# Halving the first layer's tiles at the start of a fused retention and SoLU kernel, with four output buffers and new operation orders

## The chip, the cores and the metric

The kernel runs on one core of one Trainium2 chip. The metric is the device time in microseconds (us) of one execution. Engines are named as in the profile: PE (TensorE matmul), PEld (its weight load), DVE (VectorE), ACT (ScalarE), POOL (GpSimd), SP (the engine that issues nearly all transfers).

## The reference

Eight batches of eight heads, 576 positions, head size 64; the result is then 4608 tokens of 512 numbers, which pass through two layers.

```python
scores = scale * np.matmul(q, k.transpose(0, 1, 3, 2))
ret = scores * Dmat[None]                 # Dmat: gamma_h ** (i - j) for i >= j, else 0
x = np.matmul(ret, v)                     # -> 4608 tokens x 512
h = x @ w_in                              # 512 -> 1024
e = np.exp(h - h_max); sm = e / (sum(e) + 1e-09)
solu = h * sm
ln = (solu - mu) / np.sqrt(var + 1e-06) * g_ln
out = ln @ w_out                          # 1024 -> 512
```

The kernel leaves out `h_max` and the division by the sum, which only scale a row that is normalised afterwards; a count of the sums of exponentials at the end decides whether the result holds or a general path must run.

## The kernel before

**Tiling.** The work is cut into 18 windows (a batch and 256 of its positions; the last 64 positions of four batches form one window). Each window has two halves of four heads, numbered i = 0 to 35, and two tiles of 128 tokens, numbered t = 0 to 35; window w has i and t = 2w and 2w + 1.

**Operations of a half i.** `ldq`, `ldk`, `ldv` load 256 KB each into raw buffers (five of each kind). `sq` and `sk` (L394, mostly POOL, a few on DVE) scale q and k by the decay, `cv` (L399) casts v. `T` transposes q and k on PE; `Te` or `TL` copies that to SBUF on ACT. `K` multiplies k and v for the running state, `st` (DVE, L554 to L557), `sm` (POOL, L562) and `sc` (POOL, L571) update and cast the state. `S` (L508) makes the scores in the one PSUM buffer named "s", `mask` (DVE, L540) applies the mask and frees it. `I` and `V` (L472) form the output in the one buffer named "xy", and `xe` (ACT, L576) copies it into `xT`.

**Operations of a tile t.** `M1_t` (L587) is the first layer: eight matmuls of 128x512 into the one PSUM buffer `h` of 128x1024, which spans two banks of 512 columns. `ex` (ACT, L595) takes the exponential of all 1024 columns and their sum, `so` (DVE, L605 for tiles 0 to 3, with a sum, else L610) multiplies h by it and so frees h. The variance comes from `va` (ACT, L624) and `fin` (DVE, L639) for tiles 0 to 3 and from `bnA`, `bnB` (DVE, L616) for the others, with `fx` (ACT, L633) and `rs` (POOL, L648 and L650) behind. `L` transposes the result, `Le` or `TL` copies it out. `M2_t` (L660) is the second layer, eight matmuls into a buffer "s" (some late tiles into "xy"), `oe` (ACT, L669) scales and copies it, `out` (SP) stores it. The last tile's M2 is cut in two, `M2_35` and `M3`, with `oe35` and `oz`.

**Weights.** `lwi0` to `lwi3` and `lwo0` to `lwo6` load 512 KB each. `wi` casts w_in into f16 (L706), a half on ACT (a), the other on DVE (b). `wg` (L710, L714) scales w_out, `WM` (L720) forms its mean, and `wc` (DVE, L728) subtracts it, so M2_0 needs all eight `wc`.

**What sets the order.** `plan()` (L122) lists all operations with durations, inputs and buffers. Each engine runs its own queue in order. `FIRST` (L42) gives each engine's order by hand up to about M1_14, `LAST` (L77) from about M1_32, and between them a key per operation does. `order_ops` (L233) walks the queues and gives each operation a planned start; the operations are written out by that start (L851 to L867), and matmuls on zeros (`fill`, L844) go into the planned gaps of PE ahead of M2_0. Two operations are skipped in that loop (L866) and written at the end:

```python
            if o.name not in ("oz", f"out{NT - 1}"):
                emit(o)
...
    with cmp.Else():
        o_ev(NT - 1, 1)
        store(NT - 1)
```

`cnt`, `cs` and `ci` form the count that the branch reads.

Of the kernel before, what the change touches and what calls it, by code (L numbers as in the profile page):

```python
# [17 lines left out]
for _b in range(0, B, 4):  # L18
# [9 lines left out]
    ldx=0.88, ldw=1.36, out=0.65,  # L28
# [7 lines left out]
CAP = dict(  # L36
    rawq=5, rawk=5, rawv=5, q16=3, k16=4, v16=4, ev=8, s=1, ret=2, xy=1, gg=6, gt=2, s160=4, s161=9, h=1,
    e=2, solu=4, osb=3, tl=1, tlx=2, tlT=1, tlL=1, wst=5,
# [4 lines left out]
    PE=(  # L43
# [5 lines left out]
    ),  # L49
    ACT=(  # L50
# [4 lines left out]
    ),  # L55
    DVE=(
# [5 lines left out]
    ),  # L62
    POOL=(
# [4 lines left out]
    ),  # L68
    SP=(
# [23 lines left out]
        "out27 out28 out29 out30 out31 out32 out33 out34 out35"  # L93
# [19 lines left out]
def late(t):  # L113
    return t + LAG >= 37
# [7 lines left out]
def plan():  # L122
# [42 lines left out]
    for t in range(NT):  # L165
# [20 lines left out]
        op(f"L{t}", "PE", "Lw" if early else "L", [f"so{t}"] + after, (m + 2, 0.1),  # L186
# [5 lines left out]
        op(f"M2_{t}", "PE", "M2h" if end else "M2", need, (t + LAG, 3.1), [("h" if end else "xy" if late(t) and t % 2 else "s", [f"oe{t}"])])  # L192
# [14 lines left out]
    op("G", "PE", "G", [], (-9999, 0.0), [("h", ["gc"])])  # L207
# [5 lines left out]
    op("cs", "PE", 0.1, ["cnt"], (NT + 2, 3.2), [("h", ["ci"])])  # L213
# [95 lines left out]
def kernel(  # L309
# [48 lines left out]
    se = const.tile([P, NT], FP)  # L358
# [222 lines left out]
    def mm1(t):  # L581
        w, c = divmod(t, 2)
        tk[t]["h"] = h_ps = pools["h"].tile([P, DFF], FP, tag="h", name="h_ps")
        for half in range(2):
            hh = slice(half * 512, half * 512 + 512)
            for dc in range(4):
# [5 lines left out]
    def exp_(t):
        d = tk[t]
        d["e"] = pools["e"].tile([P, DFF], FP, tag="e", name="e_sb")
        nc.scalar.activation(out=d["e"], in_=d["h"], func=ACT.Exp, accum_out=se[:, t : t + 1])  # L595

    def solu(t):
        d = tk[t]
        w, c = divmod(t, 2)
        d["solu"] = pools["solu"].tile([P, DFF], F16, tag="solu", name="solu")  # L600
        if c == 0:
            ws[w]["mv"] = pools["sml"].tile([P, 2, 2], FP, tag="mv", name="mv")
        if t in VA:
            d["su"] = pools["sml"].tile([P, 1], FP, tag="su", name="su")
            nc.vector.scalar_tensor_tensor(  # L605
                out=d["solu"], in0=d["h"], scalar=1.0, in1=d["e"], op0=ALU.mult, op1=ALU.mult,
                accum_out=d["su"],
            )
        else:
            nc.vector.tensor_tensor(out=d["solu"], in0=d["h"], in1=d["e"], op=ALU.mult)  # L610
# [9 lines left out]
    def squares(t):  # L620
# [4 lines left out]
            out=x, in_=d["solu"], func=ACT.Square, bias=d["su"], scale=-1024.0,  # L625
# [119 lines left out]
    def count_b():  # L745
        cur["cs"] = t = pools["h"].tile([P, DFF], FP, tag="h", name="cs")
        nc.tensor.matmul(out=t[0:1, 0:1], lhsT=cur["n"], rhs=small[:, 68:69], start=True, stop=True)

    def emit(o):
# [29 lines left out]
        elif k_ == "gc":  # L779
            nc.vector.tensor_copy(out=gln, in_=cur["g"][:, 0:8])  # L780
# [18 lines left out]
    with tc.manual_schedule():  # L799
# [30 lines left out]
        def busy(firsts, lasts):  # L830
# [9 lines left out]
            (lambda: pools["h"].tile([P, DFF], FP, tag="h", name="wm")[:, 0:512],  # L840
             busy(["G"], ["gc"]) + [(a, b + 0.7) for a, b in busy([f"M1_{t}" for t in n_t], [f"so{t}" for t in n_t])]),
# [119 lines left out]
```

## Time and profile before

| | us |
|---|---|
| median of three runs | 212.88 |
| lowest, highest | 212.33, 213.75 |
| the profiled execution | 212.58 |
| its span in the trace | 210.9 |
| PE busy | 200.8 (95%) |
| DVE busy | 166.1 (79%) |
| ACT busy | 141.7 (67%) |
| POOL busy | 141.7 (67%) |
| PE busy on zeros (L846, 41 matmuls into tl) | 12.7 |

Busy shares are averages over a start, in which loads arrive and PE has waits, a long middle, in which PE is full, and a short end. A slice of the page is 210.9 / 40 = 5.3 us. In a row of the timeline the numbers are start and duration, then engine, line, operation, output <- inputs, shapes and count; brackets hold the idle time before it and what ended it. `M1` starts (from the timeline): M1_0 15.59, M1_1 22.08, M1_2 28.72, M1_3 33.68, M1_4 41.33, M1_5 48.44, M1_6 53.44, M1_7 58.66, M1_8 63.83; from M1_8 on a tile takes about 4.9 to 5.1 us.

### The profile page before, as it was taken

Reading aid. Unit: us, or ns where it says so; the run is one execution under the profiler, and the core shown is the slowest. Engines: PE = TensorE matmul, PEld = TensorE weight load, DVE = VectorE, ACT = ScalarE, POOL = GpSimd, SP = SyncE. Lnnn points to the kernel's source line nnn. Section 1 sums busy time; section 2 is a strip of 40 time slices with the busy share of each in tenths; the row PEclk is TensorE's granted clock in tenths of the full one; section 3 lists DMA queues with packets and bytes.
Section 4 is the critical chain, followed back from the end, with each engine's and each line's share of the span. In section 5 each row is a group of like instructions: output and inputs, shape, how many; then the busy total and the mean of one; then the engine's idle time right before and its main releaser. Section 6 shows DMA issues by size and latency. Waiting matters only on the chain. (4 is left out here: it accounts for less than half of the span.)

```text
span 210.9 us, 10171 instructions
## 1 busy us (share of the span) xinstructions
PE 200.8 (95%) x4400; PEld 113.2 (54%) x4400; DVE 166.1 (79%) x279; ACT 141.7 (67%) x235; POOL 141.7 (67%) x240
## 2 busy tenths in 40 slices
PE   7986989999999999999999999999999999999992
PEld 2442654665566555555555555555666555554451
DVE  6565779997868898978898898889988998753760
ACT  2375787897666776776666777666767777573752
POOL 7434758999997975948787979797979792001110
PEclk9999999999999999999999999999999999999999
DMA  5999999999666559778999686776355222311224
GB/s 157 345 355 334 329 311 269 301 293 306 195 188 188 169 139 278 217 214 259 314 288 305 198 252 183 217 234 181 94 152 153 54 57 67 71 63 54 101 101 104
DMA packets 64814, 42.66 MB, mean 202 GB/s; under 512 B 3320, under 2 KB 58624, under 8 KB 64768
## 3 DMA queue, kind: packets, MB, share of 16 engines
q1 hardware_dynamic: 64528, 41.82, 68.4%
q8 instruction: 34, 0.56, 1.2%
q10 hardware_dynamic: 240, 0.18, 0.5%
q14 instruction: 12, 0.10, 0.2%
HBM read 32.55 MB, written 9.44 MB: 199 GB/s over the span
## 5 line engine op out<-in xcount | busy, mean ns | idle before, releaser
L587 PE MATMUL h_ps<-w_in,xT 128*128 128x512 f16 x288 | 68.5, 380 | 0.0
L660 PE MATMUL o_ps<-w2c,ev 128*128 128x512 f16 (+1 forms) x296 | 67.6, 373 | 0.0
L610 DVE TENSOR_TENSOR solu<-h_ps,e_sb 128x1024 f16<-128x1024 f32 x32 | 39.2, 1223 | 16.7 <-ACT e_sb L595 16.5
L595 ACT ACTIVATE e_sb<-h_ps 128x1024 f32<-128x1024 f32 x36 | 36.8, 1023 | 21.9 <-PE h_ps L587 20.4
L540 DVE TENSOR_TENSOR ret<-s_ps,masks 128x1024 f16<-128x1024 f32 x36 | 43.9, 1220 | 6.0 <-PE s_ps L508 5.4
L660 PEld LDWEIGHTS <-ev 128*128 128x128 f16 x296 | 28.7, 98 | 32.7
L616 DVE BATCH_NORM_STATS2 bs<-solu 128x6 f32<-128x512 f16 x64 | 43.6, 685 | 0.9
L587 PEld LDWEIGHTS <-xT 128*128 128x128 f16 x288 | 25.3, 98 | 29.1 <-ACT xT L576 0.8
L394 POOL TENSOR_TENSOR q<-rawq,small 128x512 f16<-128x512 f32 x34 | 35.4, 1042 | 7.3 <-DMA rawq<-in_q_dram 5.9
L669 ACT ACTIVATE o_sb<-o_ps,rs 128x512 f32<-128x512 f32 (+1 forms) x37 | 25.0, 676 | 21.8 <-PE o_ps L660 10.4
L394 POOL TENSOR_TENSOR k<-rawk,small 128x512 f16<-128x512 f32 x34 | 35.4, 1042 | 6.0 <-DMA rawk<-in_k_dram 5.9
L457 ACT COPY ev<-tl 128x1024 f32<-128x1024 f32 (+1 forms) x32 | 29.7, 932 | 4.7 <-PE tl L429 4.2
L576 ACT CAST xT<-xy 128x512 f16<-128x512 f32 x36 | 26.7, 742 | 3.0 <-PE xy L472 2.9
L571 POOL CAST sbd<-gg 64x256 f16<-64x256 f32 x64 | 25.4, 397 | 3.0
L562 POOL TENSOR_TENSOR gg<-gt,small 128x128 f32<-128x128 f32 x32 | 13.1, 409 | 16.9 <-DVE gt L557 16.5
L648 POOL TENSOR_TENSOR w<-mv,w 128x2 f32<-128x2 f32 x16 | 3.1, 194 | 27.8 <-ACT w L633 13.9
L399 POOL CAST v<-rawv 128x512 f16<-128x512 f32 x28 | 17.1, 609 | 0.2
L508 PE MATMUL s_ps<-ev 64*64 64x128 f16 x576 | 14.8, 218 | 0.3
L472 PE MATMUL xy<-ret,v 64*64 64x128 f16 x576 | 14.7, 217 | 0.0
L472 PEld LDWEIGHTS <-sbd 128*128 128x128 f16 x128 | 9.3, 98 | 9.3 <-issue 1.1
L446 PE MATMUL tl<-ident,solu 64*64 64x64 f16 x1024 | 14.2, 195 | 0.0
L846 PE MATMUL tl<-zeros 128*128 128x512 f16 x41 | 12.7, 445 | 1.3 <-DVE zeros L802 1.3
(71 smaller groups left out, 214.6 us busy)
## 6 DMA issues: line engine op xcount, KB each, us to landing
rawq<-in_q_dram SPq DMA_DIRECT2D x32, 256.0 KB, 5.1
rawk<-in_k_dram SPq DMA_DIRECT2D x32, 256.0 KB, 5.3
rawv<-in_v_dram SPq DMA_DIRECT2D x32, 256.0 KB, 5.1
out_dram<-o_sb SPq DMA_DIRECT2D x26, 256.0 KB, 3.1
out_dram<-o_sb SPq DMA_DIRECT2D x19, 128.0 KB, 2.3
wst<-in_moe_w_in_dram SPq DMA_DIRECT2D x4, 512.0 KB, 6.8
wst<-in_moe_w_out_dram SPq DMA_DIRECT2D x4, 512.0 KB, 7.1
rawq<-in_q_dram SPq DMA_DIRECT2D x16, 64.0 KB, 2.4
```

What stands on the lines that cost most here:

```text
L394: eng.tensor_tensor(out=t.rearrange("p j h d -> p h j d"), in0=st[i]["r" + nm], in1=g, op=ALU.mult)
L457: nc.scalar.copy(out=t[:, lo:hi].rearrange("p x (r w) -> p r x w", r=2), in_=tls[n].rearrange("p r x w -> p (r x w)").bitcast(FP).rearrang ...
L472: nc.tensor.matmul(start=(c, e) not in begun, stop=False, skip_group_check=True, **kw)
L540: nc.vector.tensor_tensor(out=d["ret"].rearrange("p e h j q -> p (e h) (j q)"), in0=d["s"].rearrange("p e h j q -> p (e h) (j q)"), in1=ma ...
L571: nc.gpsimd.tensor_copy(out=t[ee[e], :, :, ee[e]], in_=st[i]["gg"][ee[e]])
L576: nc.scalar.copy(out=xT[:, 2 * w : 2 * w + 2, 2 * hf : 2 * hf + 2].rearrange("p c h (q j) -> p c h j q", j=2), in_=xys[i][:, :, 0:256].rea ...
L587: nc.tensor.matmul(out=h_ps[:, hh], lhsT=xT[:, t, dc], rhs=w_in16[:, dc, hh], start=(dc == 0), stop=(dc == 3),)
L595: nc.scalar.activation(out=d["e"], in_=d["h"], func=ACT.Exp, accum_out=se[:, t : t + 1])
L610: nc.vector.tensor_tensor(out=d["solu"], in0=d["h"], in1=d["e"], op=ALU.mult)
L616: nc.vector.bn_stats(out=d["bs"][:, half], in_=d["solu"][:, half * 512 : half * 512 + 512])
L660: nc.tensor.matmul(out=o, lhsT=d["ev"][:, d["lo"] + c], rhs=w2c16[:, c, mm], start=(c == 0), stop=(c == 7))
L669: nc.scalar.activation(out=d["osb"][:, mm], in_=d["o", half], func=ACT.Copy, scale=ws[t // 2]["rs"][:, t % 2 : t % 2 + 1])
```

## The change

The first six tiles go through the first layer in two halves of 512 columns, each with its own product, exponential and multiplication: `M1_t`, `ex`, `so` for the first half and `Mb_t`, `ey`, `sp` for the second. `sg` (POOL) adds the two halves' sums. Tile 0's product is cut once more: `Ma0` does the part of heads 0 to 3 (two of the four steps) for both halves, ahead of M1_0 and Mb_0. h is one tile for the whole kernel, and the plan follows its two banks as `ha` and `hb`. There are four output buffers (`osb`) instead of three, and `FIRST` and `LAST` are new.

```diff
+NH, HX, ND = 6, 6, 1
-    ... s161=9, h=1, e=2, solu=4, osb=3, ...
+    ... s161=9, ha=1, hb=1, e=2, solu=4, osb=4, ...
```

Of `FIRST`, the stretches that the prediction uses (PE, ACT and POOL around M2_0, SP from the start):

```diff
 PE
-"... M1_3 T5 K7 T6 I4 S5 V4 T7 I5 S6 V5 T8 M1_4 I6 S7 V6 K8 T9 L2 M2_0 I7 L3 V7 K9 S8 M1_5 M2_1 I8 L4 V8 K10 S9 T10 M1_6"
-"M2_2 I9 L5 V9 S10 K11 T11 M1_7 M2_3 I10 L6 V10 S11 K12 T12 M1_8 ..."
+"K0 T0 S0 T1 K1 I0 V0 S1 T2 I1 S2 V1 K2 Ma0 M1_0 Mb_0 T3 K3 M1_1 I2 S3 V2 Mb_1 I3 V3 T4 L0 K4 S4 M1_2"
+"K6 Mb_2 L1 K5 M1_3 T5 K7 Mb_3 I4 V4 S5 WM I5 V5 T6 S6 I6 M1_4 T7 Mb_4 T8 S7 V6 K8 L2 T9 M2_0 I7 V7"
+"K9 S8 M1_5 L3 Mb_5 M2_1 L4 I8 T10 V8 S9 K10 M1_6 M2_2 I9 L5 V9 K11 S10 T11 M1_7 M2_3 I10 L6 V10 K12 T12 S11 M1_8 ..."
 ACT
+"cv0 Te0 cv1 Te1 wi0a xe0 Te2 wi1a cv2 xe1 wi2a wi3a ex0 cv3 ey0 Te3 ex1 xe2 cv4 ey1 xe3 Te4 cv6 Le0"
+"cv5 ex2 ey2 wg0 Le1 wg6 cv7 ex3 Te5 wg4 wg2 ey3 xe4 fx0 va1 xe5 Te6 va3 va0 Te7 ex4 Te8 xe6 ey4 va2 ..."
 DVE
+"... sp2 st5 wg7 wg1 st7 so3 wg5 wg3 mask5 sp3 wc6 wc1 wc3 wc4 wc2 mask6 wc5 wc7 wc0 mask7 fin0 so4 ..."
 POOL
-"... sk4 sq4 sk6 sm4 sc4 sk5 sm6 sk7 sm5 sq5 sc5 sq6 sq7 sk8 sq8 sk9 sc6 cv8 sq9 sm7 sc7 rs0 ..."
+"sk0 sk1 sm0 sc0 sq2 sm1 sc1 sq3 sm2 sc2 sq4 sm3 sc3 sk4 sq5 sk6 sm4 sg0 sk5 sk7 sc4 sm6 sm5 sc5 sm7"
+"sq6 sg1 sc6 sc7 cv8 sk8 sq7 sq8 sk9 sq9 cv9 rs0 ..."
 SP
-"ldq0 ldk0 ldv0 ldv1 ldq1 ldk1 lwi1 lwi2 lwi0 lwi3 ldk2 ldv2 ldq2 ldk3 ldq3 ldv3 lwo4 lwo0 ldk4 ldq4"
-"ldv4 lwo6 ldk6 lwo2 ldv6 ldk5 ldv5 ldk7 ldq5 ldv7 ldq6 ldk8 ldq7 ldq8 ldk9 ldv8 ldq9 ..."
+"ldv0 ldq0 ldk0 ldk1 ldq1 ldv1 ldk2 lwi0 ldq2 ldv2 lwi1 lwi2 lwi3 ldq3 ldk3 ldv3 ldq4 ldk4 ldv4 ldq5"
+"ldk6 ldv6 ldv5 ldk7 ldk5 lwo0 lwo6 ldv7 lwo4 lwo2 ldv8 ldq6 ldk8 ldq7 ldq8 ldk9 ldq9 ..."
```

`LAST`:

```diff
 PE
-"... M1_34 L32 M2_30 L33 L34 M1_35 M2_32 M2_33 L35 cs M2_34 M2_35 M3"
+"... M1_34 L32 L33 M2_30 M1_35 M2_33 M2_32 L35 L34 cs M2_35 M3 M2_34"
 ACT
-"... ex35 oe32 Le34 oe33 Le35 fx17 oe34 oe35 oz"
+"... ex35 fx16 oe33 Le35 fx17 Le34 oe32 oe35 oz oe34"
 DVE
-"... bnB34 cnt so35 bnA35 ci bnB35"
+"... so35 bnB34 cnt bnA35 bnB35 ci"
 SP
-"out27 out28 out29 out30 out31 out32 out33 out34 out35"
+"out27 out28 out29 out31 out30 out33 out32 out35 out34"
```

The functions:

```diff
+    sums = const.tile([P, 2, NT], FP)
+    se = sums[:, 0]
+    part = const.tile([P, 2, NH or 2, 2], FP)
+    h_ps = pools["h"].tile([P, DFF], FP, tag="h", name="h_ps")
...
+    def mm1(t, hs, dcs=range(4)):
+        for hh in hs:
+            for dc in dcs:
                 nc.tensor.matmul(
+                    out=h_ps[:, hh], lhsT=xT[:, t, dc], rhs=w_in16[:, dc, hh], start=(dc == 0), stop=(dc == 3)
                 )
...
+        hh = halves[half] if t < HX else slice(0, DFF)
+        acc = part[:, 0, t, half : half + 1] if t < HX else se[:, t : t + 1]
+        nc.scalar.activation(out=tk[t]["e"][:, hh], in_=h_ps[:, hh], func=ACT.Exp, accum_out=acc)
...
+    def sums_of(w):
+        nn = slice(0 if 2 * w < HX else 1, 2 if 2 * w in VA else 1)
+        tt = slice(2 * w, 2 * w + 2)
+        nc.gpsimd.tensor_tensor(out=sums[:, nn, tt], in0=part[:, nn, tt, 0], in1=part[:, nn, tt, 1], op=ALU.add)
```

`solu` is halved in the same way. The loop that skips `oz` and `out35` and the Else branch stay as they are.

More of the change, by code (lines that the diff above doesn't have):

```diff
@@ L36 @@
 CAP = dict(
-    rawq=5, rawk=5, rawv=5, q16=3, k16=4, v16=4, ev=8, s=1, ret=2, xy=1, gg=6, gt=2, s160=4, s161=9, h=1,
-    e=2, solu=4, osb=3, tl=1, tlx=2, tlT=1, tlL=1, wst=5,
+    rawq=5, rawk=5, rawv=5, q16=3, k16=4, v16=4, ev=8, s=1, ret=2, xy=1, gg=6, gt=2, s160=4, s161=9, ha=1, hb=1,
+    e=2, solu=4, osb=4, tl=1, tlx=2, tlT=1, tlL=1, wst=5,
 )
@@ L78 @@
     PE=(
-        "I34 L30 V34 S35 M1_32 I35 L31 V35 M2_28 M1_33 M2_29 M2_31 M1_34 L32 M2_30 L33 L34 M1_35 M2_32 M2_33 "
-        "L35 cs M2_34 M2_35 M3"
+        "I34 L30 V34 S35 M1_32 I35 L31 V35 M2_28 M1_33 M2_29 M2_31 M1_34 L32 L33 M2_30 M1_35 M2_33 M2_32 L35 "
+        "L34 cs M2_35 M3 M2_34"
     ),
     ACT=(
-        "oe27 xe34 ex32 Le30 Le31 oe28 xe35 ex33 fx15 oe29 ex34 Le32 oe30 Le33 oe31 fx16 ex35 oe32 Le34 oe33 "
-        "Le35 fx17 oe34 oe35 oz"
+        "fx15 oe27 xe34 ex32 Le31 oe28 xe35 ex33 oe29 Le30 ex34 Le33 oe31 Le32 oe30 ex35 fx16 oe33 Le35 fx17 "
+        "Le34 oe32 oe35 oz oe34"
     ),
     DVE=(
-        "so31 mask35 bnA31 so32 bnB31 bnA32 so33 bnB32 so34 bnA34 bnA33 bnB33 bnB34 cnt so35 bnA35 ci bnB35"
+        "so31 mask35 bnA31 so32 so33 bnA33 bnB31 bnA32 bnB33 so34 bnA34 bnB32 so35 bnB34 cnt bnA35 bnB35 ci"
     ),
@@ L168, in plan @@
         va = t in VA
-        op(f"M1_{t}", "PE", "M1", [f"xe{2 * w}", f"xe{2 * w + 1}"] + [f"wi{x}{y}" for x in range(4) for y in "ab"], (m, 1.4), [("h", [f"so{t}"])])
-        op(f"ex{t}", "ACT", "ex", [f"M1_{t}"], (m, 3.3), [("e", [f"so{t}"])])
-        op(f"so{t}", "DVE", "soA" if va else "so", [f"ex{t}"], (m, 4.56), [("solu", [f"L{t}", f"va{t}" if va else f"bnB{t}"])])
+        xs = [f"xe{2 * w}", f"xe{2 * w + 1}"] + [f"wi{x}{y}" for x in range(4) for y in "ab"]
+        out = f"sp{t}" if t < NH else f"so{t}"
@@ new lines, in plan @@
+        solu = [("solu", [f"L{t}", f"va{t}" if va else f"bnB{t}"])]
+        hs = [("ha", [f"so{t}"]), ("hb", [out])]
+        if t < ND:
+            op(f"Ma{t}", "PE", "M1h", [f"xe{2 * w}"] + [f"wi{x}{y}" for x in range(2) for y in "ab"], (m, 1.0), hs)
+            xs.append(f"Ma{t}")
+        got = ["", ""] if t < ND else hs
+        if t < NH:
+            op(f"M1_{t}", "PE", "M1q" if t < ND else "M1h", xs, (m, 1.4), [x for x in got[:1] if x])
+            op(f"Mb_{t}", "PE", "M1q" if t < ND else "M1h", [f"M1_{t}"], (m, 2.3), [x for x in got[1:] if x])
+            if t < HX:
+                op(f"ex{t}", "ACT", "exh", [f"M1_{t}"], (m, 2.5), [("e", [out])])
+                op(f"ey{t}", "ACT", "exh", [f"Mb_{t}"], (m, 3.4))
+            else:
+                op(f"ex{t}", "ACT", "ex", [f"M1_{t}", f"Mb_{t}"], (m, 3.3), [("e", [out])])
+            op(f"so{t}", "DVE", "soB" if va else "soh", [f"ex{t}"], (m, 3.3 if t < HX else 4.5), solu)
+            op(out, "DVE", "soB" if va else "soh", [f"ey{t}" if t < HX else f"ex{t}"], (m, 4.2 if t < HX else 4.7))
+        else:
+            op(f"M1_{t}", "PE", "M1h" if t < ND else "M1", xs, (m, 1.4), [x for x in got if x])
+            op(f"ex{t}", "ACT", "ex", [f"M1_{t}"], (m, 3.3), [("e", [out])])
+            op(out, "DVE", "soA" if va else "so", [f"ex{t}"], (m, 4.56), solu)
@@ L172, in plan @@
+        sums = t < HX or t < NH and va
+        if sums and c:
+            op(f"sg{w}", "POOL", "sg", ([f"ey{t - 1}", f"ey{t}"] if t < HX else []) + ([f"sp{t - 1}", f"sp{t}"] if va else []), (m, 4.9))
         if va:
-            op(f"va{t}", "ACT", "va", [f"so{t}"], (m + 1, 0.8))
+            op(f"va{t}", "ACT", "va", [f"sg{w}" if sums else out], (m + 1, 0.8))
         else:
-            op(f"bnA{t}", "DVE", "bnA", [f"so{t}"], (m + 1, 0.9))
+            op(f"bnA{t}", "DVE", "bnA", [out], (m + 1, 0.9))
@@ L185, in plan @@
         after += [f"Le{t - 2}"] if t - 2 >= NS - 6 else []
-        op(f"L{t}", "PE", "Lw" if early else "L", [f"so{t}"] + after, (m + 2, 0.1),
+        op(f"L{t}", "PE", "Lw" if early else "L", [out] + after, (m + 2, 0.1),
            [("tlL" if early else "tl" if jn else "tlx", [ev_L(t)])])
@@ L579, in x_ev @@
         )
[L581 to L586, printed above, removed]
+    halves = [slice(0, 512), slice(512, 1024)]
+    def mm1(t, hs, dcs=range(4)):
+        for hh in hs:
+            for dc in dcs:
                 nc.tensor.matmul(
-                    out=h_ps[:, hh], lhsT=xT[:, t, dc], rhs=w_in16[:, dc, hh],
-                    start=(dc == 0), stop=(dc == 3),
-                )
@@ L592, in exp_ @@
[L592 to L597, printed above, removed]
+                    out=h_ps[:, hh], lhsT=xT[:, t, dc], rhs=w_in16[:, dc, hh], start=(dc == 0), stop=(dc == 3)
+                )
+    def exp_(t, half=0):
+        if not half:
+            tk[t]["e"] = pools["e"].tile([P, DFF], FP, tag="e", name="e_sb")
+        hh = halves[half] if t < HX else slice(0, DFF)
+        acc = part[:, 0, t, half : half + 1] if t < HX else se[:, t : t + 1]
+        nc.scalar.activation(out=tk[t]["e"][:, hh], in_=h_ps[:, hh], func=ACT.Exp, accum_out=acc)
@@ L598, in solu @@
+    def solu(t, half=0):
         d = tk[t]
         w, c = divmod(t, 2)
-        d["solu"] = pools["solu"].tile([P, DFF], F16, tag="solu", name="solu")
-        if c == 0:
-            ws[w]["mv"] = pools["sml"].tile([P, 2, 2], FP, tag="mv", name="mv")
+        if not half:
+            d["solu"] = pools["solu"].tile([P, DFF], F16, tag="solu", name="solu")
+            if c == 0:
+                ws[w]["mv"] = pools["sml"].tile([P, 2, 2], FP, tag="mv", name="mv")
+        hh = halves[half] if t < NH else slice(0, DFF)
@@ L655, in mm2 @@
         nm = "xy" if half or late(t) and t % 2 else "s"
-        nm = "h" if t == NT - 1 and not half else nm
         mm = slice(256 * half, 256 * half + (256 if t == NT - 1 else DM))
-        d["o", half] = o = pools[nm].tile([P, 2, 512], FP, tag=nm, name="o_ps")[:, 0, 0 : mm.stop - mm.start]
+        if t == NT - 1 and not half:
+            o = h_ps[:, mm]
+        else:
+            o = pools[nm].tile([P, 2, 512], FP, tag=nm, name="o_ps")[:, 0, 0 : mm.stop - mm.start]
+        d["o", half] = o
         for c in range(8):
@@ L700, in g_tp @@
     def g_tp():
-        cur["g"] = t = pools["h"].tile([P, DFF], FP, tag="h", name="g_ps")
-        nc.tensor.transpose(out=t[:, 0:8], in_=g_rows, identity=small[0:8, 70:78])
+        nc.tensor.transpose(out=h_ps[:, 0:8], in_=g_rows, identity=small[0:8, 70:78])
     def w_in_cast(c, half, copy):
@@ L745, in count_b, with dcs @@
     def count_b():
-        cur["cs"] = t = pools["h"].tile([P, DFF], FP, tag="h", name="cs")
-        nc.tensor.matmul(out=t[0:1, 0:1], lhsT=cur["n"], rhs=small[:, 68:69], start=True, stop=True)
+        nc.tensor.matmul(out=h_ps[0:1, 512:513], lhsT=cur["n"], rhs=small[:, 68:69], start=True, stop=True)
+    def dcs(t):
+        return range(2 if t < ND else 0, 4)
     def emit(o):
@@ L785, in emit @@
         elif k_ == "ci":
-            nc.vector.tensor_copy(out=count, in_=cur["cs"][0:1, 0:1])
+            nc.vector.tensor_copy(out=count, in_=h_ps[0:1, 512:513])
         elif name[:2] == "wi":
```

34 lines of the change are left out of this document (17 added, 17 removed), and 49 rows, old and new, of tables (ACT, DVE, PE, POOL).

## The prediction, made before the changed kernel was run

> **What bounds the kernel now.** I read the page's slices first, then the busy time by stretch, then the timeline of the stretch where TensorE stops waiting, then the timeline of the end.
>
> ```profile
> span 210.9 us, 10171 instructions
> ...
> PE   7986989999999999999999999999999999999992
> ...
> DMA  5999999999666559778999686776355222311224
> ```
>
> TensorE (PE) is full from about the eighth slice on, and DMA is full before that. The stretches give the amounts (busy us of PE, PEld, DVE, ACT, POOL in that order, then granted clock, DMA share, GB/s).
>
> ```profile
> 20.00:25.00 5.00, 4.09 (x89) 2.60 (x88) 3.68 (x8) 3.38 (x6) 3.93 (x8) 1.00 1.14 336
> ...
> 35.00:40.00 5.00, 4.32 (x81) 2.65 (x80) 4.68 (x9) 4.61 (x10) 4.86 (x7) 1.00 1.07 287
> 40.00:45.00 5.00, 4.79 (x114) 3.33 (x114) 5.00 (x7) 4.62 (x10) 4.81 (x8) 1.00 1.18 294
> ...
> 60.00:80.00 20.00, 20.00 (x526) 11.73 (x525) 16.73 (x27) 14.12 (x24) 15.99 (x28) 1.00 0.58 168
> ```
>
> From 60 us to 205 PE idles 0.3 us in all, so the time is fixed by when PE reaches that state, plus a fixed amount of PE work, plus what follows the last matmul. The first second-layer product M2_0 (45.25) is a good mark. In both orders exactly the same PE operations stand before M2_0 (T0-T9, S0-S7, K0-K8, I and V to 6, L0-L2, the first layer of tiles 0-4, WM), so the change in its start is the change of the head. Before it DMA is full (share above 1), POOL is busy 4.8 to 4.9 of 5 us and DVE 4.7 to 5.0.
>
> ```profile
> 36.77 2.04 POOL L394 TENSOR_TENSOR q<-rawq,small 128x512 f16<-128x512 f32 x2
> 38.77 1.04 POOL L394 TENSOR_TENSOR k<-rawk,small 128x512 f16<-128x512 f32 x1
> 39.77 1.04 POOL L394 TENSOR_TENSOR q<-rawq,small 128x512 f16<-128x512 f32 x1
> 40.78 1.04 POOL L394 TENSOR_TENSOR k<-rawk,small 128x512 f16<-128x512 f32 x1
> 41.76 0.85 POOL L571 CAST sbd<-gg 64x256 f16<-64x256 f32 x2
> 42.68 0.61 POOL L399 CAST v<-rawv 128x512 f16<-128x512 f32 x1
> 43.25 1.04 POOL L394 TENSOR_TENSOR q<-rawq,small 128x512 f16<-128x512 f32 x1
> ...
> 43.90 1.22 DVE L540 TENSOR_TENSOR ret<-s_ps,masks 128x1024 f16<-128x1024 f32 x1
> ...
> 44.34 0.40 PE L419 MATMUL tl<-ident,q 128*128 128x128 f16 x4 [0.19 <-POOL q L394]
> ...
> 45.25 1.89 PE L660 MATMUL o_ps<-w2c,ev 128*128 128x512 f16 x8
> ```
>
> Rows of POOL alone, then of DVE and PE. These are sq6, sq7, sk8, sq8, sk9, sc6, cv8, sq9, mask7, T9, M2_0. POOL runs without a gap, T9 starts 0.05 us after sq9 ends (44.29), and M2_0 starts 0.13 after mask7 frees the one "s" buffer (45.12). Two waits end together there.
>
> ```profile
> 203.00 3.65 PE L660 MATMUL o_ps<-w2c,ev 128*128 128x512 f16 x24
> ...
> 205.24 1.10 ACT L669 ACTIVATE o_sb<-o_ps,rs 128x512 f32<-128x512 f32 x2 [1.19 <-POOL rs L650]
> ...
> 205.95 1.89 SPq L685 DMA_DIRECT2D out_dram<-o_sb  x3
> ...
> 206.75 0.47 ACT L669 ACTIVATE o_sb<-o_ps,rs 128x256 f32<-128x256 f32 x1 [0.41 <-PEq L916]
> 207.25 0.56 ACTq L685 DMA_DIRECT2D out_dram<-o_sb  x1
> ```
>
> At the end M2_34, M2_35 and M3 run to 206.65. oe34 (205.24) and both parts of out34 (205.95 and 206.48) are done under M3, so only oz (0.47) and one SP issue (207.37) stand behind it. That issue's last packet lands at 209.96 by the trace's landing marks.
>
> **The change, part by part.** The profiled execution took 212.58, of which 210.9 is span and 1.7 lies around it. The median of the three runs, 212.88, is 0.30 above it. The sum is made on 212.58.
>
> *Halves.* PE does the same 8 matmuls a tile. A half exp costs about 0.68: a 128x512 copy on ACT is 0.58, and the accumulator read adds about 0.10 beyond it (ex0: 1.02 and 0.20, 1.12 together). Two make 1.36 against 1.12, so +0.24 by six tiles = 1.4 us on ACT. A half product on DVE is 0.66 from start to start (wc, 128x512 from PSUM: 34.99 to 35.65), 1.3 against 1.2, plus a second accumulator read (0.08) for tiles 0 to 3: about 1 us on DVE in all. What it buys is the h cycle: M1_1 (22.08), M1_2 (28.72) and M1_3 (33.68) start after so0 (21.28), so1 (27.08) and so2 (33.63) gave h back. With two halves the PE writes one while DVE reads the other. That shortens a tile by up to 1.5 us, yet only where h is the last wait. I take it at zero at M2_0, because the next two parts end later; its cover is gone if they don't.
>
> *SP's new order.* Loads land in order of issue, at about 0.87 us per 256 KB (sq3 and cv3 started on their loads at 19.95 and 20.73) and 1.3 to 1.4 per 512 KB. q2, v2 and k2 move ahead of w_in, so w_in is complete after 4.25 MB instead of 3.5 (17.5 against 14.8 by the landing marks): tile 0's product comes 2.5 us later, with T2, S2, K2 and mask2 done under that wait. cv3 (v3 lands at 20.70 in both) now stands ahead of ey0 on ACT, so so0/sp0 end near 23. By hand from such rows, M1_1, I2, S3 and V2 are done at 24.6 against 24.9: no change. w_out is complete after 9.5 MB instead of 8.0 (35.1 against 29.7). wg2 behind it ends at 35.9, and WM at 37.5 instead of 33.5. Behind WM DVE has eight wc (0.655 each) and mask6 and mask7 (1.13 each): 7.5, so 45.1 at the earliest, as late as now. q6 becomes the 24th input load behind 8 weight loads (10.0 MB, mark 36.75); it was the 23rd (35.98).
>
> *POOL's new order.* sq6 cannot start before 36.8. POOL is by then idle (sm7 would end near 34.6), so nothing earlier is late. Behind sq6 come sg1, sc6, sc7, cv8, sk8, sq7, sq8, sk9, sq9. Steps between starts in the rows above: 1.00 for sq or sk, 0.92 for sc, 0.57 for cv8. sg1 is shown nowhere. It lies between the 128x2 operation (0.19) and the 128x128 one (0.40); I take 0.40, since it also waits for sp3 (37.8 by my count). From 36.85: 1.0 + 0.4 + 0.92 + 0.92 + 0.57 + 4 x 1.0 + 1.04 = 8.85, so sq9 ends at 45.7 instead of 44.3. sc7 and sg1 have moved ahead of it; sc7 stood behind.
>
> *PE's new order.* It puts T7, Mb_4, T8 ahead of S7. sq7 ends at 42.7, T7 runs to 43.2, Mb_4 (four matmuls, 0.87) to 44.1, T8 to 44.5, S7 to 44.9, mask7 45.0 to 46.2, and M2_0 starts at **46.3, +1.05**; T9 after sq9 gives 46.2. Then S8 must wait for oe0 (M2_0's end 48.2, plus 0.1, plus 0.69), and L3, which filled that wait, has moved behind M1_5: +0.45 (M2_1 at 51.7 against 50.18). Later K11 and K12 with T12 move ahead of S10 and S11 and fill waits that show as M1_6 to M1_7 5.22 and M1_7 to M1_8 5.17 against 4.93 later: -0.45.
>
> *The end.* M2_34 moves behind M3. PE's work is the same; M2_35 waits for Le35 about 0.1, so PE ends at 206.75. Now oe34 is last: 206.85 to 207.55. oz and out35 are left out of the ordered list and issued in the Else branch whatever the order says, so they stay behind it. SP issues out34's two parts at 207.6 and 208.1 (0.48 and 0.59), passes the branch (0.3, as from 207.07 to 207.37) and issues out35 at 209.0 against 207.37: **+1.6**. The bounds: 0.2 if out34's issues hid, 2.2 if the count, now behind bnB35, also holds PE.
>
> *osb 4, Ma0.* No wait of ACT for an output buffer shows in the groups; Ma0 lies before 20 us. Zero.
>
> Sum: 212.58 + 1.05 + 0.45 - 0.45 + 1.6 = 215.2.
>
> The Trainium skill, "DMA: Bandwidth & Descriptors" (section "Where 436 GB/s comes from"), puts the HBM limit of one core at about 358 GB/s for such transfers. Here 8.5 MB (8.9 million bytes) landed from 8.77 to 36.75, 318 GB/s, below the page's limit. By the page's rate q6 would land near 33.7 and the sum would be about 212.4, if POOL, free near 34.6, started at once; I keep the rows' rate.
>
> **The rivals.**
>
> *Loads come sooner (not slower).* The early slices move 345 and 355 GB/s, and the new order has other transfers side by side. At 350 GB/s q6 lands at 34.2, POOL starts near 34.7, 2.1 earlier, WM follows as w_out does, and M2_0 starts at 44.2: 215.2 - 2.1 = 213.1. With POOL's sm7 also earlier by the halves, 2.5 is had and the time is 212.7. It decides the sign from q6 at about 34.2. Against it: DMA share is above 1 in every stretch to 50 us and the 256 KB spacing is even.
>
> *The end costs nothing.* If out34's issues and the branch overlap, only 0.2 is left there: 213.8. For it: SP's branch took only 0.3. Against: oe34 needs M2_34, and SP issues in order.
>
> *The head is won.* T9 and M2_0 could come as early as q9's landing (41.19) allows, 1.04 for sq9 and 0.6 for T9: 42.9, -2.3, with the end's +1.6 gives 211.9, and 210.3 without. It needs POOL to have sq7, sq8 and sk9 done before 41, which its order does not allow after 36.75.
>
> *ACT becomes the bound.* It is busy 4.6 of 5 us at 35 to 45 and gains 1.4; va3 and va0 (1.25 each) stand ahead of Te7. If they end 1 us after T7, S7 and M2_0 follow: 216.2.
>
> *The halves are not told apart.* h is now one tile for the whole kernel. If a wait covers all of it, Mb waits for ex, about +0.7 for each of four tiles: up to 218.0.
>
> **How the numbers follow.** Forecast (head +1, end +1.6, 215.2): 0.50. End costs nothing (213.8): 0.12. Loads sooner (212.7 to 213.1): 0.12. Head won (210.3 to 211.9): 0.10. ACT (216.2): 0.10. Halves not apart (218.0): 0.06. The one-per-cent marks, about what a measurement of this kernel can tell from no change, are 210.75 and 215.01. Forecast cases spread by about 1 us, so some 0.34 of its 0.50 lie above 215.01. Slower: 0.34 + 0.10 + 0.06 = 0.50. Faster: most of "head won", 0.08. Within: the rest, 0.42. The range leaves out the last rival's end and the best of the head: 211.9 to 217.0. The likeliest case's own range is 214.0 to 216.3.
>
> **What would show it.** Right: sq6 starts near 36.8 straight on its load; sq9 ends near 45.7; M2_0 starts near 46.3, right behind mask7; oe34, then out34's two issues, then out35's at about 209, behind a last M2_34 that ends near 206.7 plus the head's shift. Wrong: sq6 before 35.5, POOL without a wait ahead of it, M2_0 before 45, or out35's issue within 1 us of the last matmul.

## The result, and the profile after

The changed kernel took **222.09 us** (median of 4 runs, 220.91 to 222.85) against 213.09 (median of 4 runs on the same chip): a ratio of 1.043, 95% interval [1.0385, 1.0471]. It is slower by 9.0 us, outside the predicted 211.9 to 217.0. The profiled execution took 222.49, with a span of 220.7.

The page of the changed kernel, the same lines as before and the granted clock (PEclk):

```profile
span 220.7 us, 10193 instructions
...
PE   7887777989999999999999999999999999999970
PEclk9999996999999999999999999999999999999998
DMA  6999999986368459895996866776454232211224
```

A slice is now 5.5 us. PE is less full than before in the fifth to seventh slices, about 22 to 39 us, and the granted clock falls in the seventh. From 60 us on PE is full, as before. The stretches (PE, PEld, DVE, ACT, POOL, granted clock, DMA share, GB/s):

```profile
20.00:25.00 5.00, 3.80 (x69) 2.21 (x67) 3.55 (x9) 2.84 (x7) 4.63 (x8) 1.00 0.99 282
25.00:30.00 5.00, 4.08 (x76) 2.71 (x76) 3.06 (x8) 4.18 (x11) 3.31 (x4) 1.00 0.85 257
30.00:35.00 5.00, 2.67 (x49) 1.45 (x47) 3.12 (x9) 3.01 (x9) 3.42 (x7) 0.98 1.05 370
35.00:40.00 5.00, 5.00 (x38) 2.40 (x36) 1.67 (x5) 3.61 (x7) 1.62 (x4) 0.68 1.18 296
...
60.00:80.00 20.00, 20.00 (x494) 11.40 (x492) 15.81 (x27) 13.51 (x21) 16.36 (x27) 1.00 0.59 174
```

From 20 to 35 us no engine is full, and from 35 to 40 DVE, ACT and POOL stand at 1.67, 3.61 and 1.62 of 5 us, where the kernel before had 4.68, 4.61 and 4.86. (PE's 5.00 there is at a granted clock of 0.68.) That is a chain of waits between engines, not one that is overloaded. The timeline of PE, ACT and DVE, the first layer's rows of tile 2 and the first of tile 3 (L618 is M1 and Mb, L627 ex and ey, L638 so and sp):

```profile
29.40 1.04 PE L618 MATMUL h_ps<-w_in,xT 128*128 128x512 f16 x4
...
30.61 1.04 PE L618 MATMUL h_ps<-w_in,xT 128*128 128x512 f16 x4
...
31.75 0.60 ACT L627 ACTIVATE e_sb<-h_ps 128x512 f32<-128x512 f32 x1 [1.23 <-PE h_ps L618]
...
32.47 0.69 DVE L638 SCALAR_TENSOR_TENSOR solu<-h_ps,e_sb 128x512 f16<-128x512 f32 x1 [1.04 <-ACT e_sb L627]
...
33.20 0.60 ACT L627 ACTIVATE e_sb<-h_ps 128x512 f32<-128x512 f32 x1 [0.76 <-DVE solu L638]
...
33.92 0.69 DVE L638 SCALAR_TENSOR_TENSOR solu<-h_ps,e_sb 128x512 f16<-128x512 f32 x1 [0.75 <-ACT e_sb L627]
...
34.67 1.81 PE L618 MATMUL h_ps<-w_in,xT 128*128 128x512 f16 x4 [2.33 <-DVE solu L638]
```

M1_2 ends at 30.44, but ex2, which reads only its columns, starts 0.1 us after *Mb_2* ends (31.65). ey2 reads the other bank, complete since 31.65, but starts when so2 ends (33.16). M1_3, which writes the first bank, free since so2's end at 33.16, waits for sp2 (34.62). Product, exponential and multiplication follow one another, half by half: the two halves are not told apart. PE is idle 2.33 us, the clock then drops, and M1_3's four matmuls take 1.81 us instead of 1.04.

The row that the forecast hung on, POOL's start on sq6 (starts and durations, POOL alone):

```profile
39.82 0.40 POOL L594 TENSOR_TENSOR gg<-gt,small 128x128 f32<-128x128 f32 x1 [3.04 <-DVE gt L589]
40.18 1.04 POOL L426 TENSOR_TENSOR q<-rawq,small 128x512 f16<-128x512 f32 x1
43.71 0.20 POOL L648 TENSOR_TENSOR sums<-part 128x4 f32<-128x4 f32 x1 [2.49 <-DVE solu L638]
43.85 1.74 POOL L603 CAST sbd<-gg 64x256 f16<-64x256 f32 x4
```

sq6 starts at 40.18 behind the state's update (sm7), though q6 had landed at 38.44. Behind it sg1, which took 0.20, waits 2.49 for sp3. The list from sc6 to sq9 then takes 7.5 us, as worked out. The marks along the way, from the timelines and the landing marks:

| | before | after | later by |
|---|---|---|---|
| M2_0 starts | 45.25 | 51.93 | 6.68 |
| M2_1 starts | 50.18 | 57.68 | 7.50 |
| M1_8 starts | 63.83 | 71.16 | 7.33 |
| M1_34 starts | 192.49 | 199.54 | 7.05 |
| PE ends | 206.65 | 214.25 | 7.60 |
| last landing | 209.96 | 219.53 | 9.57 |

So some 7 us are lost ahead of M2_1 and another 2.5 behind M1_34. (M1_35 is no mark for the end here: the new `LAST` moves L34, some 0.4 us of PE, from ahead of M1_35 to behind it.) The end, all engines:

```profile
212.79 1.46 PE L701 MATMUL o_ps<-w2c,ev 128*128 128x512 f16 x6
...
214.28 1.05 ACT L710 ACTIVATE o_sb<-o_ps,rs 128x512 f32<-128x512 f32 x2 [1.33 <-PE o_ps L701]
215.00 2.78 SPq L726 DMA_DIRECT2D out_dram<-o_sb  x3
215.37 0.57 ACTq L726 DMA_DIRECT2D out_dram<-o_sb  x1
```

The order is the forecast one: oe34 behind the last M2_34, out34's two issues (215.00 and 215.53), the branch, out35's issue at 217.31. PE had also waited 0.59 us for Le35 ahead of M2_35, and the second issue of out34 took 1.48 instead of 0.59.

### The profile page after: what moved, and what is told of

Same layout as the page of the kernel before. It is cut to its first block, busy times and chain, and to the rows that moved or that the text cites. A ratio compares the mean times of both kernels' runs of the same rounds, so it can differ in the third digit from the quotient of the medians.

```text
span 220.7 us, 10193 instructions
## 1 busy us (share of the span) xinstructions
PE 203.3 (92%) x4405; PEld 114.1 (52%) x4405; DVE 167.2 (76%) x289; ACT 142.7 (65%) x247; POOL 143.9 (65%) x243
## 5 line engine op out<-in xcount | busy, mean ns | idle before, releaser
L618 PE MATMUL h_ps<-w_in,xT 128*128 128x512 f16 x288 | 70.1, 383 | 5.0 <-DVE solu L638 2.3
L701 PE MATMUL o_ps<-w2c,ev 128*128 128x512 f16 (+1 forms) x288 | 66.7, 376 | 0.0
L627 ACT ACTIVATE e_sb<-h_ps 128x1024 f32<-128x1024 f32 (+1 forms) x42 | 37.9, 903 | 29.7 <-PE h_ps L618 23.5
L643 DVE TENSOR_TENSOR solu<-h_ps,e_sb 128x1024 f16<-128x1024 f32 (+1 forms) x34 | 39.2, 1156 | 15.4 <-ACT e_sb L627 15.3
L618 PEld LDWEIGHTS <-xT 128*128 128x128 f16 x288 | 25.6, 98 | 33.4 <-issue 6.1
L710 ACT ACTIVATE o_sb<-o_ps,rs 128x512 f32<-128x512 f32 (+1 forms) x36 | 24.5, 683 | 21.6 <-PE o_ps L701 11.1
L603 POOL CAST sbd<-gg 64x256 f16<-64x256 f32 x64 | 26.1, 408 | 3.0
L594 POOL TENSOR_TENSOR gg<-gt,small 128x128 f32<-128x128 f32 x32 | 13.8, 432 | 16.7 <-DVE gt L589 16.0
L891 PE MATMUL tl<-zeros 128*128 128x512 f16 x46 | 13.8, 429 | 1.3 <-DVE zeros L846 1.3
L688 POOL TENSOR_TENSOR rs<-w,small 128x2 f32<-128x2 f32 x18 | 12.4, 691 | 1.6 <-DVE w L677 0.4
```

The source lines that it names most:

```text
L603: nc.gpsimd.tensor_copy(out=t[ee[e], :, :, ee[e]], in_=st[i]["gg"][ee[e]])
L618: nc.tensor.matmul(out=h_ps[:, hh], lhsT=xT[:, t, dc], rhs=w_in16[:, dc, hh], start=(dc == 0), stop=(dc == 3))
L627: nc.scalar.activation(out=tk[t]["e"][:, hh], in_=h_ps[:, hh], func=ACT.Exp, accum_out=acc)
L643: nc.vector.tensor_tensor(out=d["solu"][:, hh], in0=h_ps[:, hh], in1=d["e"][:, hh], op=ALU.mult)
L701: nc.tensor.matmul(out=o, lhsT=d["ev"][:, d["lo"] + c], rhs=w2c16[:, c, mm], start=(c == 0), stop=(c == 7))
L710: nc.scalar.activation(out=d["osb"][:, mm], in_=d["o", half], func=ACT.Copy, scale=ws[t // 2]["rs"][:, t % 2 : t % 2 + 1])
```

## The experiments

The theory after this look: h is one tile, a wait on it covers both banks, and this makes the halves serial. The rival: the new orders cost it, whatever the halves do. All but one of the kernels compute everything as the changed one does or as the one before does; the exception only adds matmuls on zeros.

**1. Halves told apart.** For tiles 0 to 5 h becomes two tiles of one bank; later tiles use one tile of two banks. The orders stay.

```diff
-    h_ps = pools["h"].tile([P, DFF], FP, tag="h", name="h_ps")
+    hx = [pool_h.tile([P, 512], FP, tag=f"hh{x}", name="h_ps") for x in range(2)]
...
-                    out=h_ps[:, hh], lhsT=xT[:, t, dc], ...
+                    out=h_of(t, hh), lhsT=xT[:, t, dc], ...     # hx[half] for t < 6
```

> The changed kernel, but for the first six tiles h lies in two tiles of one bank each instead of one tile of two banks (one tile again from tile 6 on). All orders stay. Theory A, the waits follow h as a whole, so the halves run one after another (ex0 waits for Mb_0, ey0 for so0, M1_1 for ey0): the cycle of a tile falls from 5.3 us to about 3, M2_0 comes 4 to 5 us sooner and the time is 216.5 to 218.5; the rest is the orders' +1 and the end's +2.5. Rival B, the new orders cost the head whatever the halves do: 221 to 222.5, within 1 us of the changed kernel.

Measured: 217.56 us (216.31 to 217.82), ratio 1.021 [1.0151, 1.027]. The group of the first layer on PE, of the changed kernel and then of this one (the last column is idle time ahead of it, and what ended it):

```profile
L618 PE MATMUL h_ps<-w_in,xT 128*128 128x512 f16 x288 | 70.1, 383 | 5.0 <-DVE solu L638 2.3
```

```profile
L630 PE MATMUL h_ps<-w_in,xT 128*128 128x512 f16 x288 | 69.3, 380 | 0.0
```

The 5.0 us of waits are gone, and so is the drop of the clock. POOL in this run:

```profile
37.02 1.04 POOL L428 TENSOR_TENSOR q<-rawq,small 128x512 f16<-128x512 f32 x1 [2.42 <-DMA rawq<-in_q_dram]
38.02 0.20 POOL L660 TENSOR_TENSOR sums<-part 128x4 f32<-128x4 f32 x1
38.15 1.75 POOL L605 CAST sbd<-gg 64x256 f16<-64x256 f32 x4
...
44.55 1.04 POOL L428 TENSOR_TENSOR q<-rawq,small 128x512 f16<-128x512 f32 x1
```

The last mask ahead of M2_0 (DVE), and M2_0 (PE):

```profile
44.97 1.23 DVE L574 TENSOR_TENSOR ret<-s_ps,masks 128x1024 f16<-128x1024 f32 x1 [1.04 <-PE s_ps L542]
...
46.25 0.81 PE L713 MATMUL o_ps<-w2c,ev 128*128 128x512 f16 x3
```

sq6 starts straight on its load, sq9 ends at 45.59, mask7 at 46.19, and M2_0 starts at 46.25: the head of the prediction. The theory holds: under these orders one tile for two banks costs 4.5 us. Runs 6 and 7 below differ in the tiles of h alone as well, and their medians are 4.3 apart. e and solu stayed one tile each, and here ey2 writes its half of e from 29.04 while so2 (28.99 to 29.68) reads the other, so it is h alone. Why the program tells the halves of e apart and not those of h, no run shows.

**2. No halves.** The changed kernel with whole tiles: `NH, HX, ND = 0, 0, 0`.

> The changed kernel with no tile halved and no early share of tile 0 (the three counts set to 0); new orders and four output buffers stay. Theory A: the serial halves are gone, products as in the kernel before, so the head is later by the orders alone, +1 to +2, with the end's +2.5: 216 to 217.5. Rival B: 220 to 222.

Measured: 219.37 us (219.0 to 220.27), ratio 1.0319 [1.0261, 1.0377], which neither side expected. M2_0 starts at 48.18. The new orders with whole tiles cost 6.2 us; with serial halves 9.0; with halves told apart 4.4. So the orders do need halves, and real ones (with Ma0, which this run leaves out too) are worth 1.8 us there, while those that were written cost another 2.7.

**3. The end alone.** The kernel before with the new `LAST`.

> The kernel before with only the new order of the end. If the end is a cost of its own (oe34 last, its two stores issued ahead of out35): 215.0 to 215.8, +2 to +2.6, in the profile all behind the last matmul and in front of M2_35. If the end's extra time in the changed kernel was a consequence of the head: 212.8 to 213.5.

Measured: 215.56 us (214.95 to 216.78), ratio 1.0124 [1.007, 1.0179]. PE's row of M2_35 and M3, and what follows:

```profile
205.37 3.63 PE L660 MATMUL o_ps<-w2c,ev 128*128 128x256 f16 x24 [0.84 <-DVE count L786]
```

```profile
209.09 1.05 ACT L669 ACTIVATE o_sb<-o_ps,rs 128x512 f32<-128x512 f32 x2 [2.12 <-PEq L916]
209.80 1.89 SPq L685 DMA_DIRECT2D out_dram<-o_sb  x3
```

From PE's end (209.00) to out35's issue (211.22) it is 2.2 us against 0.7 before, so SP's part is the 1.5 to 1.6 of the prediction. PE's wait of 0.84 for the count is the term that was set at 0.1. In this execution PE also stood still 1.11 us near 109.7, which has nothing to do with the end.

**4. Halves in the old order.** The changed kernel's functions, both orders those of before with each second half right behind its first, Ma0 off; the three new sums and two ScalarE items (va2, fx1) placed by me.

> The first six tiles halved as in the changed kernel (h one tile), tile 0 not cut further, but all orders as before, each second half put right behind its first; sums, va2 and fx1 placed where their inputs allow. Theory A: the serial halves cost the head 3 to 6 us with the old orders too, and the end costs nothing: 216 to 219. Rival B: 213 to 214.5.

Measured: 215.46 us (215.22 to 215.74), ratio 1.0125 [1.0075, 1.0176]. Neither side expected it: serial halves cost less in the old order. M2_0 starts at 46.45 and M2_1 at 52.36. In this profile, too, the granted clock falls to 0.50, from 19.53 to 22.94 us.

**5. Does the low clock cost?** Eight matmuls on zeros ahead of M1_3.

```diff
+            if o.name == "M1_3":
+                fill(tl1[0].bitcast(FP), 8)
```

> The changed kernel, with eight more 512-column matmuls on zeros put ahead of M1_3, into the left bank of the tile of transposes, so that TensorE is not idle while M1_3 waits for the halves of tile 2. Nothing else differs. Theory: the late halves cost twice, by the wait (2.33 us of idle TensorE) and by the clock of 0.50 that follows it, in which M1_3 took 1.81 instead of 1.04, the two transposes .63 instead of .40 each and the fill 1.55 instead of 1.03, together about 1.7 us, of which the transposes and M1_3 (1.2) lie on the chain: the clock stays at 0.9 or more, and the time is 220.4 to 221.4. Rival: the lower clock lies beside VectorE's and ScalarE's chain and costs nothing: 221.8 to 222.4.

Measured: 221.98 us (220.59 to 223.38), ratio 1.0422 [1.0366, 1.0478]. The rival holds as to the time. The trace shows the edit at work: the clock is 1.00 from 35 to 40 us, M1_3 takes 1.02, and M2_0 starts at 49.99, 1.94 sooner than in the profiled execution of the changed kernel. In this execution PE also stood still for 2.4 us (1.01 near 109, 0.38 and 1.02 near 170 and 176), so its own 223.38 does not show the gain. The medians leave nothing of it. The mean granted clocks of this run's four executions (0.995, 0.995, 0.992, 0.997) lie above those of three of the changed kernel's four (0.989, 0.980, 0.996, 0.987), so the drop is rarer here, and this kernel loses as much elsewhere; where, the one trace does not show beyond the stops.

**6. The end undone.** The changed kernel with the old `LAST`.

> The changed kernel with the last part's orders of before, all else as changed. Theory: the end costs by itself what it cost in the kernel before, 215.56 less 213.13 or 2.4 us: 219.2 to 220.2. Rival: the end's cost depends on how late the head is, and part of the 9.2 us is counted twice: 220.6 to 222.3, or under 219.

Measured: 220.78 us (219.2 to 221.1), ratio 1.0395 [1.035, 1.044]: 1.3 us better than the changed kernel, at the low edge of the rival. Its stretch from 35 to 40 us, and its M1_3:

```profile
35.00:40.00 5.00, 4.90 (x74) 2.47 (x72) 3.33 (x9) 4.33 (x11) 2.78 (x5) 1.00 1.15 294
```

```profile
34.39 1.02 PE L618 MATMUL h_ps<-w_in,xT 128*128 128x512 f16 x4 [2.33 <-DVE solu L638]
```

The same wait of 2.33 us, in the same order, without the drop of the clock, and M2_0 at 49.98. So the drop does not come in every execution. But it is not confined to the profiled one either. One drop, 3.4 us at 0.50, takes 0.008 off an execution's mean granted clock, and the low clock behind the last matmul takes off at most 0.010 in any of the traces (run 2). The changed kernel's execution of 222.85 us, at 0.980, needs a drop ahead of that; the one of 220.91, at 0.996, has no room for one. Run 6's profiled execution (219.20 us, clock 1.00) is likewise its fastest, the others (0.988 to 0.992) took 220.33 to 221.10. Without the drop the serial halves cost 49.98 less 46.25, or 3.7 us, at M2_0, or 3.0 against run 7, which has the same head as run 1 and starts M2_0 at 47.01.

Why only 1.3 came back: the last store of this run took 3.5 us from issue to landing. The row of the issue list, of before, of the changed kernel, and of this run:

```profile
out_dram<-o_sb ACTq DMA_DIRECT2D x1, 128.0 KB, 2.4
```

```profile
out_dram<-o_sb ACTq DMA_DIRECT2D x1, 128.0 KB, 2.8
```

```profile
out_dram<-o_sb ACTq DMA_DIRECT2D x1, 128.0 KB, 3.5
```

All six runs with the old `LAST` and the changed functions (4, 6 to 9 and 11) have 3.4 to 3.9 there; the others have 2.3 to 2.8. The traces point to a cause. The page's queue "q8 instruction", by its name that of program code, has 34 packets of 16 KB in the kernel before and in runs 3 and 10, and 35 in all others. In the six runs the last of them starts 1.0 to 1.4 us after that issue and takes 0.88 to 1.28 us, and the store's last five packets, of more than 200, end 0.8 to 1.2 us after the rest; before and run 10 have no such packet there. No run moves that packet, so this is not shown by an experiment.

**7. Halves told apart, and the old `LAST`.**

> The first layer's result of tiles 0 to 5 in two tiles of one bank, and the last part's orders of before; the head's orders and the four output buffers as changed. Theory (serial halves 4.5, end 2.4, head's orders the rest): 217.56 less 2.4, so 214.6 to 215.7, which leaves 1.5 to 2.5 us for the head's orders. Rival: with the halves told apart the end no longer costs what it cost alone: 216.3 to 217.8.

Measured: 216.47 us (215.43 to 216.9), ratio 1.0175 [1.0121, 1.0229], at the low edge of the rival's range. Against 217.56 this is 1.1 better, and again the last store took 3.9 us. Of the 3.7 us over before, M2_0 has 1.76 (it starts at 47.01), the way to M2_1 0.33, and the end 1.3 (from M1_35 to the last landing 14.05 against 12.74).

**8 and 9. Halves told apart in the old order.** Run 4 with two tiles for h; then the same with va2 put back behind Te5.

```diff
-... ey3 Te5 Te6 xe4 fx0 Te7 xe5 va0 Te8 ex4 ey4 xe6 Le2 va2 fx1 va3 oe0 ...
+... ey3 Te5 va2 Te6 xe4 fx0 Te7 xe5 va0 Te8 ex4 ey4 xe6 Le2 fx1 va3 oe0 ...
```

> Halves told apart (two tiles of one bank for tiles 0 to 5) in the order of before, each second half right behind its first, no share of tile 0 ahead, the last part's order of before, four output buffers. Theory (what costs in halves is that they are serial, and with the order of before that is the 2.3 us of the run with one tile of h): 213.0 to 214.4. Rival: the halves cost by their number of instructions and by my placing of two ScalarE items ahead of oe0, whether told apart or not: 215.0 to 216.0.

Measured: 215.31 us (214.93 to 216.59), ratio 1.0124 [1.008, 1.0168]: the rival.

> The run with halves told apart in the order of before, with one ScalarE item put back where the kernel before has it: va2 behind Te5 instead of ahead of oe0. Theory: the 1.1 us that this run lost between the first and the second output tile (M2_1 at 51.30, before 50.18) came from that item, and with it gone halves told apart cost nothing in the head: M2_1 at 50.1 to 50.5, and the time 213.6 to 214.8, what is left over 212.9 being at the end (the last store took 1 us longer from issue to landing in all runs with the last order of before and the changed code). Rival: the halves themselves cost it, by 0.2 us more of ScalarE and of VectorE for each of six tiles: M2_1 at 51.0 or later and 215.0 to 215.8.

Measured: 216.04 us (214.6 to 217.03), ratio 1.0145 [1.0069, 1.0221]. The placing did cost (from M2_0 to M2_1 it is 4.92 us again, 5.88 in run 8), but the time is no better, so the theory falls; the rival has M2_1 right (51.23) and the time 0.2 too low. M2_0 started at 46.31, against 45.42 in run 8. In this execution PE also stood still for 1.41 us near 110. In the old order, halves gain nothing, told apart or not (215.46, 215.31, 216.04): the three kernels are 2.3 to 3.3 us slower than before, and the separate tiles of run 8 make no difference to run 4. So the 4.5 us belong to the new orders and the one tile together.

**10. Four buffers alone.** The kernel before with `osb=4`.

> The kernel before with four output buffers instead of three, and nothing else. Theory: no item of before waits for an output buffer on the path, so 212.3 to 213.3. Rival: the fourth buffer moves the last tile's stores to another place and is what makes the last landing late in the runs with four buffers and the old last order: 213.7 to 214.4, and the last store takes 3.3 us or more from issue to landing instead of 2.4.

Measured: 213.27 us (212.36 to 214.64) against 212.78, ratio 1.0018 [0.999, 1.0046]: no difference. The fourth buffer is not what delays the last store in runs 4 and 6 to 9 (2.8 us here).

**11. The old order of loads under the new head**, halves told apart, old `LAST`.

> As the run with halves told apart, the changed head and the last order of before, but with the queue of loads in the order of before. Theory: what the changed head costs with halves told apart is GpSimd's row waiting for q6's load (2.65 us of idle GpSimd ahead of sq6 in that run); with the order of before q6 comes about 1.5 us sooner, GpSimd's row starts by 36.5, M2_0 is at 45.2 to 46.0, and the time is 214.8 to 215.9. Rival: other loads (k and q of tiles 4 and 5, w_out) come later in that order and hold up TensorE or GpSimd before q6's row, so nothing is won: M2_0 at 46.5 or later, 216.2 to 218.

Measured: 233.3 us (231.93 to 234.93), ratio 1.0933 [1.0864, 1.1002], beyond both. From its list of waits (us in total, times, longest):

```profile
POOL q L425 <- DMA rawq<-in_q_dram: 14.0, 3, 6.3
POOL k L425 <- DMA rawk<-in_k_dram: 12.9, 3, 9.9
...
DVE k L425 <- DMA rawk<-in_k_dram: 6.8, 1, 6.8
```

M2_0 starts at 56.18. The engines' order and the loads' order are one: the new POOL order takes sq5 ahead of sk6, sk5 and sk7, while the old order of loads brings q5 behind all three, so POOL stands idle 5.7 us in front of a load that is not there. That is 9.2 of the 16.8 us over run 7. The rest comes later: POOL waits 9.88 us for a k (to 101.58), the 9.9 of the second row, and PE stands 5.60 us (99.23 to 104.83). The run does not answer what it was made for.

## Why the prediction was wrong

*The step that failed* is the halves: "That shortens a tile by up to 1.5 us, yet only where h is the last wait. I take it at zero at M2_0". They cost 3.0 to 3.7 us at M2_0 without the drop of the clock (49.98 against 47.01 and 46.25) and 4.5 of the time (222.09 against 217.56), in which the drop has a share in some executions. The text had the mechanism among its rivals, as "the halves are not told apart", with a chance of 0.06 and a price of 0.7 us for each of four tiles, up to 218.0. Both were too low. The change itself said that h is one tile for the whole kernel. Only the plan follows its two banks, and a plan's buffers set the order in which operations are written, not the waits. That deserved the largest chance of all. And the price: the text had Mb waiting for ex. In the trace Mb_2 is done first and ex2 waits for it, ey2 waits for so2, and the next tile's product for sp2. M1_2 to M1_3 took 5.27 us (29.40 to 34.67), with PE at 2.67 of 5.

The Trainium skill, "Perfetto Trace Analysis" (section "Matmuls"), says that independent groups of matmuls should rotate through different PSUM banks, so that ACT and DVE empty one while the next is written. Here two banks were used in turn, and the steps of the two halves did not overlap until each bank was a tile of its own.

*SP's and POOL's orders* were right once this wait was gone. Forecast: sq6 at 36.8 on its load, sq9's end 45.7, mask7's 46.2, M2_0 46.3. Run 1: 37.02, 45.59, 46.19, 46.25. Only sg1 was mis-sized, 0.40 against 0.20. That M2_0 is met to 0.05 is partly luck: sq6 came 0.17 later than the 36.85 of the sum, and sg1 made up for it. Run 7, the same head, has sq6 at 37.80, again on its load, and M2_0 at 47.01; the head of before starts M2_0 at 45.25, 45.69 (run 3) and 45.93 (run 10).

*S8's wait* was forecast at +0.45 at M2_1; run 1 has 5.26 from M2_0 to M2_1 against 4.93, so +0.33.

*The later gain* of 0.45 is smaller: from M2_1 to M1_8 the changed kernel makes up 0.17 and run 1 0.18.

*The end* was forecast at +1.6, bounds 0.2 to 2.2; alone it costs 2.4 (run 3; 1.9 from M1_34 to the last landing), and from M1_34 to the last landing the changed kernel takes 2.5 us more. The mechanism was right and, in run 3, SP's part too; in the changed kernel out34's second issue takes 0.9 longer. Mis-sized was PE's wait: 0.84 for the count in run 3, and 0.59 for Le35 in the changed kernel, against 0.1. The count's wait was named as the upper bound and then left out.

*osb 4 at zero* was right (run 10).

*The 212.4* that the text gives beside its own sum does not follow from its numbers: with POOL free at 34.6, only 2.2 us come off 215.2, which gives 213.0. q6 landed at 36.95 in run 1 and at 38.44 in the changed kernel, so keeping the rows' rate was right.

*The sum.* On the medians, halves not told apart cost 4.5 us and the end 2.4 as run 3 has it, or 1.1 to 1.3 as runs 6 and 7 give it back. The rest of the 9.0, some 2 us by the first and 3.2 to 3.4 by the second, goes with the head's orders; of it 1.0 stands at M2_0 and 0.3 more at M2_1 in run 1 (1.8 and 0.3 in run 7).

*Open.* Even with the halves told apart the kernel takes 217.56, above the range. Of its 4.4 us over before the traces place 3.3 (1.0 at M2_0, 0.3 more at M2_1, 2.2 behind M1_34, less 0.2 in between); 1.1 is not placed, though its profile has a PE stop of 1.38. Open too are what the clock's drop takes from the medians, and by experiment the causes named above for the last store and below for PE's stops.

## What to carry to other kernels

Ask of every buffer that is to be used in parts what the wait covers: a plan or an order that treats two banks as two buffers gains nothing as long as the program waits on them as one tile. Here it lost 4.5 us under the new orders. When a rival follows from a line of the diff and not from a guess about the chip, it gets the largest chance, and its price is worked out through the whole cycle of waits. Orders written by hand for several queues over the same stretch are one object: the loads' order put back alone (run 11) costs 16.8 us over run 7, more than the whole change.

## What the runs showed of the hardware that was not expected

After 2.33 us of idle PE (32.35 to 34.67) the granted clock was 0.50 from 34.77 to 38.18 us in one execution, and 1.00 in another with the same wait (run 6). M1_3 took 1.81 against 1.02. The Trainium skill, "TensorE: Matmul & The Clock Gate" (section "HAM oscillation — how this bites in real kernels"), gives as a rule that no gap in PE's work should be longer than about 3.4 us. The gap here is shorter, and yet it sufficed.

What decides is where the wait falls. In each trace the changes of the granted clock lie a whole number of 3.41 us steps apart: in the changed kernel at 34.77, 38.18 and, behind the last matmul, 219.09. PE's busy time in such steps, and the clock in the step behind:

| run | step, us | PE busy, us | clock behind it |
|---|---|---|---|
| changed kernel, the whole wait in one step | 31.35 to 34.77 | 1.09 | 0.50 |
| run 6, the same wait across two | 29.89 to 33.30 | 2.17 | 1.00 |
| | 33.30 to 36.71 | 2.32 | 1.00 |
| run 4 | 16.11 to 19.53 | 1.29 | 0.50 |
| run 10 | 18.20 to 21.61 | 1.54 | 1.00 |

Over all thirteen traces, some 800 steps, 0.50 followed wherever PE was busy 1.39 us or less, and 1.00 wherever it was busy 1.52 us or more. So a wait of some 2 us costs the clock or not by its place alone, and that place differs from execution to execution.

PE stops of 1.0 to 1.4 us that the profile puts down to "issue" come in the middle of the kernel in five of the thirteen profiles (runs 1, 3, 5, 8 and 9), at another place in each (104 to 121 us, and 176); shorter ones of 0.2 to 0.5 us are in eight, runs 5 and 8 among them. From 50 to 205 us that makes fifteen, and all end 1.26 to 1.52 us after a 16 KB packet of the queue "q8 instruction" ended, while such packets come some 5 us apart. So PE seems to wait there for program code, which no run tests by a change. The longer stops are as large as the terms of the sum, so a difference of 1 us between two single profiles says little before they are taken off.
